# One arm for single shapes in the routed 256-token units: inner branches, moved row turns, split fills and apart last scatters

## The chip, the core and the metric

The kernel runs on one core of a Trainium2 chip. The core has a matrix engine (TensorE, PE in the profile, with PEld for its weight loads), a vector engine (VectorE, DVE), a scalar engine (ScalarE, ACT), GpSimd (POOL) and SyncE (SP), which issues most of the transfers. Each engine has its own instruction stream, and they meet at semaphores. The metric is the device time of one execution in microseconds (us); lower is better.

## What is computed

Three layers follow one another: attention between tokens and states in both directions, a dense feed-forward layer with the mish function, and a layer of eight experts of which each token takes one. The change touches the last:

```python
def _moe2_ref(x, expert_emb, tau, w1, w2):
    xn = x / (np.linalg.norm(x, axis=-1, keepdims=True) + 1e-06)
    en = expert_emb / (np.linalg.norm(expert_emb, axis=-1, keepdims=True) + 1e-06)
    logits = xn @ en.T / tau
    expert_idx = np.argmax(logits, axis=1)
    ...
    gate_w = probs[np.arange(N), expert_idx]
    out = np.zeros((N, D), dtype=np.float32)
    for e in range(E):
        mask = expert_idx == e
        if not mask.any():
            continue
        h = np.maximum(x[mask] @ w1[e], 0.0)
        out[mask] = gate_w[mask, None] * (h @ w2[e])
    return out.astype(np.float32)
```

There are 2304 tokens of 512 numbers, and an expert's w1 is 512 x 1024, its w2 1024 x 512.

## The kernel before

All products are made from two parts of each number, a high and a low one: high by high, high by low and low by high. The routing is worked out on the chip, which sorts the tokens by expert and cuts them into **units** of up to 256 tokens of one expert. Units 0 and 1 are interleaved with the end of the dense layer and the planning; units 2 to 12 run in a loop that is unrolled in the program, each with its own code on each engine. Unit 12 is END; a few more units exist for other routings and are skipped here.

A unit has a *kind*, read from a planned table into a register of each engine. Kind 2 (double) has two blocks of 128 tokens; kind 1 (thick) one block; kind 0 (half) at most 64 tokens, whose high and low parts lie side by side in one block, so that two products suffice and are added at the end. In the profiled execution units 2, 5, 6, 7, 10 and 12 are double, 3, 4, 8, 9 and 11 half, and none is thick. `chosen` is an If over the kind with three arms, once for `up` and once for `out_of`.

The stages of unit U, in program order:

- `gather(U + 2)`: GpSimd issues two indirect transfers (L1052) that fetch the rows `xg` of unit U + 2. It stands behind the scatters of unit U - 1 in GpSimd's queue.
- `up`: the product with w1 into three PSUM tiles `hp`. In a double unit that is four groups of 24 matmuls. In a half unit it is two groups of eight matmuls of 512 columns (`high`, L1173); ScalarE copies each to `hs` (L1216), TensorE turns it with four matmuls against `fold` (L1222, "turn" below; `fold` adds the two halves), and `positive` makes hth (ScalarE L1140, VectorE L74). Near its end, `xt_turns(U + 1)` (L1085) turns the rows of the next unit by eight transposes.
- `next_rows`: ScalarE and VectorE split the turned rows into xth and xtl, then `fill` and `fill_soon` split staged weights: ScalarE writes w1h or w2h (L79), VectorE w1l or w2l (L80), four tiles for w1 and four for w2, according to the planned code `due`. For unit 2 it asks for w1 and w2 of unit 3, for unit 3 for w1 of unit 5, for unit 8 for w2 of unit 9, for unit 9 for w1 and w2 of unit 10. Then `kinds` loads kinds of later units to registers (L1063).
- `out_of`: the product with w2 into `y` (`down` in a double unit, 48 matmuls; 16 matmuls in a half one), `scale` on VectorE (L66), in a half unit a copy of the other lanes on ScalarE (L1243) and an addition on VectorE, and `scatter` on GpSimd (L1155), an indirect transfer to the output.
- `fetch`: SyncE loads the staged weights of later units (L972, L975).

Each engine works through its own stream in order. Scatters of unit END are not issued in the unit but at the very end of the program, after the join of all branches. Between units 0 and 1, `placed` contains the matmuls po (L736) that find each token's place; `group(1, 0)` and `group(1, 1)` before and after it are products of unit 1 (hp, L111 to L113).

Of the kernel before, what the change touches and what calls it, by code (L numbers as in the profile page):

```python
# [21 lines left out]
P = 128  # L22
# [33 lines left out]
def body(tc, x, state, w_in, w_out, ee, tau, w1, w2, out):  # L56
# [58 lines left out]
    with stack:  # L115
# [861 lines left out]
        def split_all(U, parts=(1, 2)):  # L977
            for part in parts:
                for i in range(4):
                    split(*weights(U, part, i), staged[part, i])  # L980
# [73 lines left out]
        kind, kf, due_, hT, HP = {}, {}, {}, [], P // 2  # L1054
        fold = dots.rearrange("p t e -> p (t e)")[:, 0:HP]

        def kinds(U, flag=False):
# [111 lines left out]
        def high(o, terms, last):  # L1169
            n = len(terms)  # L1170
            for low in range(2):
                for k, (h, _, *w) in enumerate(terms):
                    T.matmul(o, h, w[low], start=not low and k == 0, stop=last and bool(low) and k == n - 1)  # L1173

        def low(o, terms):
            n = len(terms)
            for k, (_, l, wh, _) in enumerate(terms):
                T.matmul(o, l, wh, start=False, stop=k == n - 1)

        def sums(o, terms, thick):  # L1180
            high(o, terms, not thick)
            if thick:
                low(o, terms)

        def chosen(U, pieces, do):

            def arm(n):
                for j in range(pieces):
                    do(U, n, j)
# [9 lines left out]
        def up(U, n, j):  # L1199
            def rows_of_next():  # L1200
                if U + 1 in xo:
# [378 lines left out]
```

## Time and profile before

| what | us |
|---|---|
| median of 3 runs (lowest to highest) | 697.71 (697.35 to 698.95) |
| profiled execution | 695.59 |
| its span | 693.8 |
| TensorE busy in the span | 659.0 |
| VectorE busy | 482.6 |
| ScalarE busy | 438.2 |
| GpSimd busy | 184.8 |

The profile comes from one execution. The busy table gives each engine's work; the waits name what ended the idle time before an instruction ("issue" is idle time for which no semaphore stands); the timeline lists instructions in order of start, runs of like ones joined. In a timeline row the first number is the start, the second the time to the end of the group, then engine, line, operation, tile written <- tiles read, shape and count; the bracket at the end is the idle time before it and what ended it. Matmul records overlap: the step from one start to the next is the cost. Rows with a "q" behind the engine are of its sequencer, which reads ahead of the engine.

### The profile page before, as it was taken

Reading aid. Unit: us, or ns where it says so; the run is one execution under the profiler, and the core shown is the slowest. Engines: PE = TensorE matmul, PEld = TensorE weight load, DVE = VectorE, ACT = ScalarE, POOL = GpSimd, SP = SyncE. Lnnn points to the kernel's source line nnn. Section 1 sums busy time; section 2 is a strip of 40 time slices with the busy share of each in tenths; the row PEclk is TensorE's granted clock in tenths of the full one; section 3 lists DMA queues with packets and bytes.
Section 4 is the critical chain, followed back from the end, with each engine's and each line's share of the span. In section 5 each row is a group of like instructions: output and inputs, shape, how many; then the busy total and the mean of one; then the engine's idle time right before and its main releaser. Section 6 shows DMA issues by size and latency. Waiting matters only on the chain. (4 is left out here: it accounts for less than half of the span.)

```text
span 693.8 us, 11871 instructions
## 1 busy us (share of the span) xinstructions
PE 659.0 (95%) x3833; PEld 564.2 (81%) x3833; DVE 482.6 (70%) x1044; ACT 438.2 (63%) x771; POOL 184.8 (27%) x165
## 2 busy tenths in 40 slices
PE   8797999999999999999999999999999999989994
PEld 8787986777888888888887877988978899878893
DVE  5988698889657686686769878897556732467630
ACT  5776998989788867766786677531535521365410
POOL 2776265555000030030004041042121122121101
PEclk9999999999999999999999999999999999999998
DMA  7654044442010154541121354624677281464300
GB/s 182 166 156 122 9 147 125 142 126 62 1 60 1 42 150 97 110 85 38 61 63 49 112 190 162 173 77 158 224 264 280 81 306 62 140 201 175 137 4 34
DMA packets 58243, 82.78 MB, mean 119 GB/s; under 512 B 25050, under 2 KB 35802, under 8 KB 58148
## 3 DMA queue, kind: packets, MB, share of 16 engines
q1 hardware_dynamic: 54388, 70.31, 33.9%
q0 software_dynamic: 3760, 11.30, 5.0%
q8 instruction: 47, 0.77, 0.4%
q14 instruction: 48, 0.39, 0.2%
HBM read 65.32 MB, written 13.65 MB: 114 GB/s over the span
## 5 line engine op out<-in xcount | busy, mean ns | idle before, releaser
L111 PE MATMUL acc<-woh,gh 128*128 128x512 f32 x272 | 108.6, 403 | 3.3 <-ACT gh L79 3.2
L112 PE MATMUL acc<-wol,gh 128*128 128x512 f32 x272 | 107.4, 396 | 0.0
L113 PE MATMUL acc<-woh,gl 128*128 128x512 f32 x272 | 94.0, 399 | 0.9 <-DVE gl L80 0.8
L113 PE MATMUL hp<-xth,w1l 128*128 128x256 f32 x256 | 72.3, 282 | 1.2 <-DVE w1l L80 1.2
L111 PE MATMUL hp<-xth,w1h 128*128 128x256 f32 x256 | 72.3, 282 | 0.5 <-DVE htl L74 0.5
L112 PE MATMUL hp<-xtl,w1h 128*128 128x256 f32 x256 | 72.1, 282 | 0.6 <-DVE xtl L80 0.6
L111 PEld LDWEIGHTS acc<-woh,gh 128*128 128x128 f32 x272 | 51.2, 188 | 16.4 <-ACT gh L79 6.5
L522 ACT ACTIVATE er<-h,mb__104 128x512 f32<-128x512 f32 x68 | 46.5, 684 | 25.5 <-PE h L113 22.0
L113 PEld LDWEIGHTS acc<-woh,gl 128*128 128x128 f32 x272 | 50.5, 188 | 14.8 <-DVE gl L80 4.1
L1140 ACT ACTIVATE hth<-hp 128x512 fp32r<-128x512 f32 (+1 forms) x34 | 17.8, 533 | 66.3 <-PE hp L113 58.6
L112 PEld LDWEIGHTS acc<-wol,gh 128*128 128x128 f32 x272 | 51.2, 188 | 10.1
L1155 POOL DMA_INDIRECT out<-ys,ix x19 | 19.1, 1007 | 150.3 <-DVE ix L1158 70.2
L528 DVE TENSOR_TENSOR er<-er 128x512 f32<-128x512 f32 x56 | 40.3, 719 | 22.4 <-ACT er L522 21.9
L551 ACT ACTIVATE h<-er,mb__104 128x512 f32<-128x512 f32 x68 | 47.3, 695 | 8.3 <-DVE er L528 4.8
L111 PE MATMUL h<-xh,mh 128*128 128x512 f32 x128 | 51.3, 401 | 0.1
L112 PE MATMUL h<-xl,mh 128*128 128x512 f32 x128 | 50.7, 396 | 0.4 <-DVE xl L80 0.4
L113 PE MATMUL h<-xh,ml 128*128 128x512 f32 x128 | 50.5, 394 | 0.0
L552 ACT ACTIVATE er<-er,mb__104 128x512 f32<-128x512 f32 x68 | 49.3, 726 | 1.4
L113 PEld LDWEIGHTS hp<-xth,w1l 128*128 128x128 f32 x256 | 48.4, 189 | 1.8 <-DVE w1l L80 1.8
L112 PEld LDWEIGHTS hp<-xtl,w1h 128*128 128x128 f32 x256 | 48.3, 189 | 1.2 <-DVE xtl L80 0.8
L111 PEld LDWEIGHTS hp<-xth,w1h 128*128 128x128 f32 x256 | 48.3, 189 | 1.1 <-DVE htl L74 0.7
L523 ACT ACTIVATE u<-h 128x512 f32<-128x512 f32 x68 | 40.3, 593 | 0.0
(481 smaller groups left out, 1716.1 us busy)
## 6 DMA issues: line engine op xcount, KB each, us to landing
w<-in_moe_w_in SPq DMA_DIRECT2D x16, 512.0 KB, 3.9
w<-in_moe_w_out SPq DMA_DIRECT2D x16, 512.0 KB, 3.6
es<-in_moe_w SPq DMA_DIRECT2D x32, 256.0 KB, 3.1
sg<-in_moe_w SPq DMA_DIRECT2D x12, 512.0 KB, 3.7
sd<-in_moe_w SPq DMA_DIRECT2D x12, 512.0 KB, 6.5
se<-in_moe_w SPq DMA_DIRECT2D x12, 512.0 KB
xn<-in_x SPq DMA_DIRECT2D x32, 128.0 KB, 3.1
md<-mr SPq DMA_DIRECT2D x28, 128.0 KB, 2.4
```

Of the source, the lines that this page charges most:

```text
L111: T.matmul(o, lh, rh, start=first, stop=False)
L112: T.matmul(o, lh, rl, start=False, stop=False)
L113: T.matmul(o, ll, rh, start=False, stop=last)
L522: A.activation(z, h, AF.Tanh, scale=0.5, bias=mb_[:, 0:1])
L523: A.activation(u, h, AF.Silu)
L528: V.tensor_tensor(out=z, in0=z, in1=z, op=ALU.mult)
L551: A.activation(r, z, AF.Square, scale=QS, bias=mb_[:, 1:2])
L552: behind["ACT"] = A.activation(z, z, AF.Square, scale=QS, bias=mb_[:, 2:3])
L1140: A.activation(hi, i, AF.Relu)
L1155: G.indirect_dma_start(out=out[:, :], out_offset=bass.IndirectOffsetOnAxis(ap=ix_[U][r], axis=0), in_=ys_[U][r], in_offset=None, bounds_ch ...
```

## The change

The thick and the half shape now share an arm: `chosen` has two arms, double and single. In the single arm the matmuls with low parts (`low`), and the choice between transposes and turns with `fold`, stand in small branches of their own. Where the inner branch of `low` is not taken, one matmul of one column with a tile of zeros stands in its place. For these branches TensorE has a second register with the kind, `kp`. The order in the single arm is new: the first turn lies after five of the second group's eight matmuls, the second turn among the first half of the y matmuls, which begin before it.

The turns of the next unit's rows stand at the head of the unit, and if the next unit is not double only those of the first block are made. `fill` is cut in two: the first part (all of w1 for the next unit, half of its w2, or half of the w1 for the unit after) stays in the middle, the second stands after the scatters. Half of `group(1, 1)` moves ahead of `placed`. In unit END the second half's product and scale stand in an If of their own behind the arm.

The diff, cut to its core:

```diff
-        def fill(U):
+        def fill(U, half):
             with tc.If(due_[U] > 1):
-                with tc.If(due_[U] > 2):
-                    split_all(U + 1, [1])
-                split_all(U + 1, [2])
-
-        def fill_soon(U):
-            with tc.If(due_[U] == 1):
-                split_all(U + 2, [1])
+                if not half:
+                    with tc.If(due_[U] > 2):
+                        split_all(U + 1, 1)
+                split_all(U + 1, 2, range(2 * half, 2 * half + 2))
+            if U + 2 <= END:
+                with tc.If(due_[U] == 1):
+                    split_all(U + 2, 1, range(2 * half, 2 * half + 2))
...
                 kind[U] = nc.values_load(cell, engines=UENG, min_val=0, max_val=2)
+                kp[U] = nc.values_load(cell, engines=[ET.PE], min_val=0, max_val=2)
...
         def xt_turns(U, parts=range(2)):
-            for r in range(2):
+            def rows_of(r):
...
+            rows_of(0)
+            if U not in kp:
+                rows_of(1)
+                return
+            with tc.If(kp[U] > 0) as w:
+                rows_of(1)
+            with w.Else():
+                T.matmul(xo[U][1][:, 511:512], wz, wz[:, 0:1], start=True, stop=True, skip_group_check=True)
...
+        def low(U, o, terms):
             n = len(terms)
+            with tc.If(kp[U] > 0) as w:
+                for k, (_, l, wh, _) in enumerate(terms):
+                    T.matmul(o, l, wh, start=False, stop=k == n - 1, skip_group_check=True)
+            with w.Else():
+                T.matmul(o[:, 0:1], wz, wz[:, 0:1], start=False, stop=True, skip_group_check=True)
+
+        def chosen(U, j):
             with tc.If(kind[U] > 1) as w:
-                arm(2)
+                (double_up, double_out)[j](U)
             with w.Else():
-                with tc.If(kind[U] > 0) as v:
-                    arm(1)
-                with v.Else():
-                    arm(0)
+                (single_up, single_out)[j](U)
...
+        def double_out(U):
+            for r in range(1 if U == END else 2):
+                down(U, [r])
+                scale(U, r)
+                scatter(U, r)
...
+            high(hq[U][0], terms(0), True)
+            low(U, hq[U][0], terms(0))
+            leave(0)
+            high(hq[U][1], terms(1), True, range(5))
+            turn(0)
+            high(hq[U][1], terms(1), False, range(5, 8))
+            low(U, hq[U][1], terms(1))
+            leave(1)
+            high(y, ts[0:4], True, range(4))
+            turn(1)
+            high(y, ts[0:4], False, range(4, 8))
+
+        def single_out(U):
+            o, ts = y_[U][0], second(U)
+            high(o, ts[4:8], False)
+            low(U, o, ts)
             scale(U, 0)
...
             group(1, 0)
+            group(1, 1, [0])
             placed()
...
             grouped(1, 0)
-            group(1, 1)
+            group(1, 1, [1])
...
-                    chosen(U, 4, up)
-                    next_rows(U)
+                    if U < END:
+                        xt_turns(U + 1)
+                    chosen(U, 0)
+                    middle(U)
                     if U < END:
                         ends(U)
-                    chosen(U, 2, out_of)
+                    chosen(U, 1)
+                    if U < END:
+                        fill(U, 1)
+                    else:
+                        with tc.If(kind[U] > 1):
+                            down(U, [1])
+                            scale(U, 1)
```

`leave(m)` is the copy to hs on ScalarE, `turn(m)` the four turns and `positive`, and `middle` is the old `next_rows` with the first part of `fill`.

On TensorE, between units 0 and 1, before: the last matmuls of `group(1, 0)` (tile hp_5123) and then those of po.

```order
L111 MATMUL hp_5123<-xth_4981,w1h_4815 128x256
L112 MATMUL hp_5123<-xtl_4982,w1h_4815 128x256
L113 MATMUL hp_5123<-xth_4981,w1l_4816 128x256
L111 MATMUL hp_5123<-xth_4981,w1h_4872 128x256
L112 MATMUL hp_5123<-xtl_4982,w1h_4872 128x256
L113 MATMUL hp_5123<-xth_4981,w1l_4873 128x256
L736 LDWEIGHTS Q
L736 MATMUL po<-ph_5007,Q 128x64
```

The same place after: hp_5124 is the tile of `group(1, 1)`; the last six of its twelve matmuls there are shown.

```order
L111 MATMUL hp_5124<-xth_4981,w1h_4815 128x256
L112 MATMUL hp_5124<-xtl_4982,w1h_4815 128x256
L113 MATMUL hp_5124<-xth_4981,w1l_4816 128x256
L111 MATMUL hp_5124<-xth_4981,w1h_4872 128x256
L112 MATMUL hp_5124<-xtl_4982,w1h_4872 128x256
L113 MATMUL hp_5124<-xth_4981,w1l_4873 128x256
L736 LDWEIGHTS Q
L736 MATMUL po<-ph_5007,Q 128x64
```

Twelve matmuls that stood behind po now stand ahead of it.

On VectorE, around the end of unit 3, before: four splits of w1, then the scale ys of the unit (first that of the double arm, then those of the thick and the half one).

```order
L80 TENSOR_TENSOR w1l_4804<-sg_5331,w1h_4803 128x1024
L80 TENSOR_TENSOR w1l_4810<-sg_5334,w1h_4809 128x1024
L80 TENSOR_TENSOR w1l_4816<-sq,w1h_4815 128x1024
L80 TENSOR_TENSOR w1l_4873<-sr,w1h_4872 128x1024
L1040 UNCONDITIONAL_BRANCH x2
L1028 UNCONDITIONAL_BRANCH
L1191 COMPARE_AND_BRANCH
L1158 CAST ix_6435<-gg_5643 128x1
L66 TENSOR_SCALAR ys_6437<-y_6139,gg_5643 128x512
```

The same place after, from the scale of the single arm on; the splits of sg stand ahead of it as before.

```order
L66 TENSOR_SCALAR ys_6422<-y_6139,gg_5665 128x512
L1253 COMPARE_AND_BRANCH
L74 SCALAR_TENSOR_TENSOR ys_6422<-hs_6147,gg_5665,ys_6422 64x512
L1253 UNCONDITIONAL_BRANCH x2
L1193 UNCONDITIONAL_BRANCH
L1032 COMPARE_AND_BRANCH
L80 TENSOR_TENSOR w2l_4676<-se_5333,w2h_4675 128x1024
L80 TENSOR_TENSOR w2l_4710<-se_5336,w2h_4709 128x1024
L1032 UNCONDITIONAL_BRANCH x2
L1038 COMPARE_AND_BRANCH
L80 TENSOR_TENSOR w1l_4816<-sq,w1h_4815 128x1024
L80 TENSOR_TENSOR w1l_4873<-sr,w1h_4872 128x1024
```

The splits of sq and sr, and the last two of w2 where these are due, have moved behind the scale.

On GpSimd, at the end of the program, before: the last two scatters and what follows, with their waits.

```order
L1549 UNCONDITIONAL_BRANCH
L1155 DMA out_0<-yse0_10163,dots_183 2176x512 [waits DMASW4_49,DMASW3_49,DMASW5_49,DMASW2_49,DMASW6_49,DMASW1_49,DMASW7_49,DMASW0_49,DVE_49]
L1155 DMA out_0<-yse1_10164,dots_183 2176x512 [waits DMASW3_49,DMASW2_49]
L1576 UNCONDITIONAL_BRANCH
L1576 ISA [waits barrier_Pool_Activation_PE_DVE_SP_gather]
```

After:

```order
L1570 UNCONDITIONAL_BRANCH
L1163 DMA out_0<-yse0_9854,dots_183 2176x512 [waits DMASW4_49,DMASW3_49,DMASW5_49,DMASW2_49,DMASW6_49,DMASW1_49,DMASW7_49,DMASW0_49,DVE_49]
L1163 DMA out_0<-yse1_9855,dots_183 2176x512 [waits DMASW3_49,DMASW2_49,DVE_49]
L1597 UNCONDITIONAL_BRANCH
L1597 ISA [waits barrier_Pool_Activation_PE_DVE_SP_gather]
```

The order is the same; the second scatter has got a wait for VectorE of its own.

## Rows read from the trace of the kernel before

**Rows 1.** The page's busy table: busy us, share of the span, instructions.

```profile
PE 659.0 (95%) x3833; PEld 564.2 (81%) x3833; DVE 482.6 (70%) x1044; ACT 438.2 (63%) x771; POOL 184.8 (27%) x165
```

**Rows 2.** Waits of TensorE, 480 to 694 us: releaser, total, times, longest.

```profile
PE hp L1173 <- issue: 3.2, 2, 1.7
PE hp L1173 <- DVE w1l L80: 1.5, 1, 1.5
PE hp L113 <- DVE w1l L80: 1.2, 3, 0.5
```

**Rows 3.** Timeline of the end of unit 12: scales and scatters.

```profile
678.00 0.75 DVE L66 TENSOR_SCALAR yse<-y,gg 128x512 f32<-128x512 f32 x1 [4.56 <-PE y L113]
...
683.58 0.75 DVE L66 TENSOR_SCALAR yse<-y,gg 128x512 f32<-128x512 f32 x1 [4.77 <-PE y L113]
684.61 0.98 POOL L1155 DMA_INDIRECT out<-yse,dots  x1 [20.46 <-DVE yse L66]
687.94 0.98 POOL L1155 DMA_INDIRECT out<-yse,dots  x1 [2.35 <-DMA out<-yse,dots]
```

**Rows 4.** Sequencer rows (ns min/median/max), 540 to 544 us; unit 5's first y.

```profile
L1063 PEldq TENSOR_LOAD <-ctl x2: 296/296/297, 541.5 to 542.2; - x2
L1191 PEldq COMPARE_BRANCH  x2: 73/186/298, 541.1 to 542.9; - x2
...
543.10 0.48 PE L111 MATMUL y<-w2h,hth 128*128 128x512 f32 x1
```

**Rows 5.** Timeline of TensorE at po.

```profile
460.22 0.28 PE L112 MATMUL hp<-xtl,w1h 128*128 128x256 f32 x1
460.34 0.28 PE L113 MATMUL hp<-xth,w1l 128*128 128x256 f32 x1
461.92 0.66 PE L736 MATMUL po<-ph,Q 128*128 128x64 bf16 x17 [1.30 <-DVE ph L66]
```

**Rows 6.** Timeline of units 8 and 9: turns, row turns, copies, splits.

```profile
605.02 1.00 PE L1222 MATMUL hp<-dots,hs 128*128 128x64 f32 x8
...
605.85 1.04 PE L1085 MATMUL gt<-ident,xg 128*128 128x128 f32 x8
...
606.53 0.42 DVE L74 SCALAR_TENSOR_TENSOR hth<-hp,hth 128x256 fp32r<-128x256 f32 x1 [4.30 <-ACT hth L1140]
...
606.74 1.00 PE L1222 MATMUL hp<-dots,hs 128*128 128x64 f32 x8
...
610.59 1.98 ACT L79 ACTIVATE w2h<-se 128x1024 fp32r<-128x1024 f32 x2
...
615.91 0.59 ACT L1243 ACTIVATE hs<-y 64x512 f32<-64x512 f32 x1 [3.34 <-DVE ys L66]
...
616.53 0.60 ACT L1216 ACTIVATE hs<-hp 128x512 f32<-128x512 f32 x1
...
617.33 1.00 PE L1222 MATMUL hp<-dots,hs 128*128 128x64 f32 x8
```

**Rows 7.** Windows of units 3, 4, 8, 9: length, engines' busy times, clock.

```profile
506.80:517.29 10.49, 10.45 (x57) 8.37 (x55) 2.51 (x9) 3.29 (x8) 3.00 (x3) 1.00 0.90 320
518.78:530.91 12.13, 10.59 (x57) 8.68 (x57) 8.20 (x14) 7.27 (x12) 3.62 (x4) 1.00 0.92 337
601.28:611.79 10.51, 10.47 (x57) 8.36 (x55) 4.17 (x9) 5.42 (x10) 2.97 (x3) 1.00 0.44 153
613.49:623.93 10.44, 10.40 (x57) 8.62 (x57) 6.24 (x12) 6.02 (x10) 2.94 (x3) 1.00 0.71 233
```

**Rows 8.** Unit 2's second scatter, unit 5's gather, their transfers' time.

```profile
503.81 2.35 DVE L80 TENSOR_TENSOR w2l<-se,w2h 128x1024 fp32r<-128x1024 f32 x2
...
514.84 1.00 POOL L1155 DMA_INDIRECT out<-ys,ix  x1 [6.35 <-DVEq L1033]
...
517.44 2.02 POOL L1052 DMA_INDIRECT xg<-x1d,perm  x1 [0.30 <-PE y L1173]
...
xg<-x1d,perm POOLq DMA_INDIRECT x2, 7.2
```

**Rows 9.** Sequencer row of TensorE at the end of unit 3.

```profile
L1191 PEldq COMPARE_BRANCH  x1: 3827/3827/3827, 514.3 to 514.3; - x1
```

More of the change, by code (lines that the diff above doesn't have):

```diff
@@ L975, in fetch_part, with split_all @@
                     Y.dma_start(staged[2, i].rearrange("p (t d) -> p t d", t=2), src)
[L977 to L980, printed above, removed]
+        def split_all(U, part, tiles=range(4)):
+            for i in tiles:
+                split(*weights(U, part, i), staged[part, i])
         def expert(s, engines):
@@ L1167, in lanes, with high @@
             return t.rearrange("p (k t) -> p k t", t=P)[:, :, half * HP : (half + 1) * HP]
-        def high(o, terms, last):
+        def high(o, terms, first, steps=None):
             n = len(terms)
[L1171 to L1175, printed above, removed]
+            for i in steps or range(2 * n):
+                h, _, *w = terms[i % n]
+                T.matmul(o, h, w[i // n], start=first and not i, stop=False, skip_group_check=True)
@@ L1218, in up @@
-            for k in range(4):
-                if n:
-                    T.transpose(tr[:, k * P : (k + 1) * P], h[:, k * P : (k + 1) * P], ident)
-                else:
-                    T.matmul(tr[:, k * P : k * P + HP], h[:, k * P : (k + 1) * P], fold, start=True, stop=True)
-            if n:
-                positive(hth[U][m], htl[U][m], tr)
-            else:
-                positive(lanes(hth[U][m], 0), lanes(hth[U][m], 1), lanes(tr, 0))
-            if j == 2:
-                rows_of_next()
@@ L1230, in out_of @@
-        def out_of(U, n, j):
-            if n > 1:
-                down(U, [j])
-                scale(U, j)
-                scatter(U, j)
-                return
-            if j:
-                return
-            q, o = U % 2, y_[U][0]
-            sums(o, [(hth[U][k // 4][:, k % 4 * P : (k % 4 + 1) * P], htl[U][k // 4][:, k % 4 * P : (k % 4 + 1) * P], W2H[q, k // 2][:, k % 2, :], W2L[q, k // 2][:, k % 2, :]) for k in range(NFE)], n)
+        def double_out(U):
[3 more added lines that the diff above has]
+                scatter(U, r)
@@ new lines, in second, with single_up, terms, leave @@
+        def second(U):
+            q = U % 2
+            return [(hth[U][k // 4][:, k % 4 * P : (k % 4 + 1) * P], htl[U][k // 4][:, k % 4 * P : (k % 4 + 1) * P], W2H[q, k // 2][:, k % 2, :], W2L[q, k // 2][:, k % 2, :]) for k in range(NFE)]
+        def single_up(U):
+            q, y, ts = U % 2, y_[U][0], second(U)
+            h, tr = hs_[U], (hq[U][2], hq[U][0])
+            def terms(m):
+                fs = slice(m * 512, (m + 1) * 512)
+                return [(*(wide2(t[U][k // 2])[:, k % 2, 0:P] for t in (xth, xtl)), W1H[q, k][:, fs], W1L[q, k][:, fs]) for k in range(KT)]
+            def leave(m):
+                A.activation(h[m], hq[U][m], AF.Copy)
+            def turn(m):
+                with tc.If(kp[U] > 0) as w:
+                    for k in range(4):
+                        T.transpose(tr[m][:, k * P : (k + 1) * P], h[m][:, k * P : (k + 1) * P], ident)
+                with w.Else():
+                    for k in range(4):
+                        T.matmul(tr[m][:, k * P : k * P + HP], h[m][:, k * P : (k + 1) * P], fold, start=True, stop=True)
+                with tc.If(kf[U] > 0) as w:
+                    positive(hth[U][m], htl[U][m], tr[m])
+                with w.Else():
+                    positive(lanes(hth[U][m], 0), lanes(hth[U][m], 1), lanes(tr[m], 0))
+            high(hq[U][0], terms(0), True)
[9 more added lines that the diff above has]
+            high(y, ts[0:4], False, range(4, 8))
@@ L1507, in body @@
             kinds(2)
-            next_rows(1)
+            middle(1)
             store(1)
+            fill(1, 1)
             fetch(1)
@@ L1540, in body @@
                         fetch_part(e, part)
-                    split_all(U)
+                    for part in (1, 2):
+                        split_all(U, part)
                     xt_tiles(U)
```

41 lines of the change are left out of this document (8 added, 33 removed).

## Prediction

> **What bounds the kernel now.** I read the busy table first, then the waits of TensorE in the stage of the 256-token units (480 to 694 us), then the timeline where units meet and where the program ends. TensorE is busy for 95% of the span [rows 1]. From 480 us on its waits are few: two stalls put down to "issue" (3.2 us), and waits for split weights of 1.5 and 1.2 us [rows 2]. So in this stage a microsecond that TensorE gains or loses reaches the end, and after TensorE's last matmul at about 683.5 us only the tail counts: scale, scatter, transfer. The profiled execution took 695.59 us, of which 693.8 us are the span; the median of the runs shown is 697.71 us, 2.12 us more. I make the sum against 695.59 and add the same 2.12 at the end.
>
> **The tail.** Unit 12 is a double one: its first half of 128 rows is scaled at 678.00, its second at 683.58 [rows 3]. Still both scatters leave after the second: GpSimd issues the first at 684.61, having waited 20.46 us for VectorE, and the second at 687.94, having waited for the first's transfer [rows 3]. In the order of the new kernel the second scatter has a wait of its own for VectorE, so the first waits for its own scale only. It then leaves at about 678.00 + 0.75 + 0.28 = 679.03, where 0.28 is the step from the end of the second scale (683.58 + 0.75 = 684.33) to 684.61. With the same 3.33 us from issue to issue (687.94 - 684.61) GpSimd is free at 682.36, before 684.61. The second scatter takes the first's place: **-3.33 us**, with 2.25 us of cover. The new branch between the halves is read by TensorE's sequencer ahead of its queue, so I count it at nothing; without that cover it is one taken branch, at most 0.3 us [rows 4]. The bounds are 0 and -3.33.
>
> **The placement matmuls.** At 461.92 TensorE starts po after idling 1.30 us for ph on VectorE [rows 5]. Twelve hp matmuls are moved ahead of it, 0.12 us apart [rows 5], 1.43 us in all, so they fill the hole, and po starts when it did. No wait of TensorE lies between 462 and the first unit's end that could swallow the gain: **-1.30 us** (bounds 0 and -1.30).
>
> **Register loads.** Each `kinds` now loads the kind twice on TensorE. A load, its check and its move take 0.7 us start to start on the sequencer (two of them from 541.5 and 542.2) [rows 4]. In unit 5 the compare that follows starts at 542.9 and lasts up to 298 ns, and y starts at 543.10 [rows 4]: there is no slack. Units 2 and 5 read two kinds each, so two more loads. In a double unit the sequencer is some 2 us ahead (first branch at 541.1, y at 543.10), which the loads and branches use up: **+1.4 us each**. Units 6 and 7 read one kind: the slack was 0.7 us and one more load uses it, 0. In half units the queue ahead is longer (512-column matmuls at (683.58 - 678.00)/24 = 0.23 us): 0. The bounds for each of the two units are 0 and 1.4; I take 1.4 because of the missing slack.
>
> What the trace shows of such a load is 296 ns, then 146 to 151 ns more and a check. The Trainium skill ("Runtime: NRT & Kernel Launch", section Instruction fetch mechanics) puts a register load at about 200 ns; by that figure alone, an estimate from the page, each unit would lose 0.4 us and the forecast would be some 2 us lower. The trace disagrees with it here, and I follow the trace.
>
> **Row turns.** They move to the head of the unit, and only four of eight remain where the next unit is a half one. Eight cost 606.74 - 605.85 = 0.89 us [rows 6]. The next unit is a half one in units 2, 3, 7, 8 and 10: -0.44 us in each. That gives unit 2 +0.95 with its loads and **unit 7 -0.44**.
>
> **Body of a half unit.** Before, U8 takes 10.51 us [rows 7]: 16 hp and 16 y matmuls at 0.23 (7.44), two turns at 605.85 - 605.02 = 0.83, row turns 0.89, so waits of about 0.5. New are three one-column matmuls where the inner branch is not taken. No such row stands in the trace; one lies between 0 and the 0.23 of a 512-column one, and I take 0.1, since the turn's short ones take 0.83/8. Branches on the sequencer are 73 to 298 ns [rows 4], five pairs in 10 us, hidden by the queue. From a turn's start to its hth the trace has 606.53 + 0.42 - 605.02 = 1.93 us [rows 6]. After turn(0) TensorE now has 0.83 + 3 x 0.23 + 0.1 = 1.6 us of work, after turn(1) 0.83 + 4 x 0.23 = 1.76: waits of 0.3 and 0.2, as much as before. So a half unit gains 0.44 and pays 0.3 (-0.15) before a half one, and pays 0.3 before a double one. **Unit 11: +0.4** (its next is double).
>
> **Units 8 and 9.** Before, TensorE's stall at the start of unit 9 (611.79 to 613.49 [rows 7]) cost less than it looks, for turn(0) of unit 9 waited on ScalarE anyway: hs of the left half of hp at 616.53 + 0.60, turn(0) at 617.33 [rows 6], which is 5.54 us after unit 8's last y. ScalarE was late because L1243 waits for VectorE's scale [rows 6], which stands behind the w2l splits. Now two of the four splits come after the scatter, so on ScalarE two w2h (2.0 us [rows 6]) stand between L1243 and that hs. Counted from the end of unit 8's turn(1): VectorE ends xth and two w2l at about 4.9 (0.38 for hth, 0.9 for xth, 2.0 for w2h, then VectorE's part); the scale takes 0.75, L1243 0.6, w2h 2.0, hs 0.6, hand-overs 0.25, so turn(0) is possible at 9.1. y ends at 3.0 (12 matmuls, 0.3 of rest), so turn(0) comes 6.1 us after it: +0.56. The rest of unit 9 was 623.93 - 617.33 = 6.60 and is now the sum of its pieces, 6.76. With unit 8's -0.15: **+0.6 us**. The removed stall does not come back as a gain.
>
> **Units 3 and 4.** The pair took 530.91 - 506.80 = 24.11 us, units 8 and 9 took 22.65 [rows 7]. By the pattern above the new pair would take 23.2, -0.9. But two things are late here. The staged weights arrive late, and the row turns of unit 5 now stand first in unit 4, at about 517. Their rows are fetched by the gather at 517.44, which follows the second scatter at 514.84; the transfers take 7.2 us in the middle [rows 8], so the rows are there at about 524.6; behind the row turns the whole unit 4 is queued on TensorE. That scatter in turn waits for the first, and the first for a scale that stands behind w2l, which ends at 503.81 + 2.35 [rows 8]. Two of these splits, 2.36 us, now come after the scale, so the gather leaves some 2.4 us earlier, and more if its scatter meets fewer weight loads: about 518 to 523. ScalarE allows turn(0) at about 524 anyway, 3.1 us after the row turns (eight hp, a small one, five hp), and the last four row turns take 0.44: this covers rows landing up to 520.5. I take **+0.3 us**, between -0.9 and +4.4 (gather no earlier than before).
>
> **Unit 10.** Weights for it are split in unit 9 and TensorE waited for them (1.2 us [rows 2]). The splits now start 3.0 instead of 4.1 us before the end of y, four row turns (0.44) fill part: the wait grows 0.6, eight turns go (-0.89), four come (+0.44): **+0.15 us**.
>
> **Sum.** -1.30 + 0.95 + 0.3 + 1.4 - 0.44 + 0.6 + 0.15 + 0.4 = +2.06 on TensorE, -3.33 in the tail: -1.27. The profiled execution becomes 694.3, the median 696.4 us. TensorE's end moves from 683.5 to about 685.6.
>
> **Rivals.** (A) The costs are covered: loads at nothing (-2.8), no late ScalarE in units 4 and 9 (-0.6 and -1.2). For it: the queue ahead of the sequencer may be deeper in the new order, and the row turns no longer stand at its end. Against: the y start right behind the compare [rows 4]. 696.4 - 4.6 = 691.8. (B) Slower: unit 4 waits at its head for the gathered rows of unit 5. If they land at 524.6 as before, turn(0) comes at 528.1, 4.1 us past my figure: 700.5. It decides from a landing after 520.5 on. For it: the transfers ran while weight loads filled the DMA queues; against: the earlier scale. (C) The change doesn't do what it says, the first last-half scatter still waits for both: without -3.33, 699.7. Against it stands the second scatter's own wait in the order. (D) A jump over the double arm waits for its code: the branch at 514.3 took 3827 ns where others took 73 to 298 [rows 4, 9], and TensorE stood 1.5 us. If units 3, 8 and 11 paid that too, 4.5 us: 700.9. Against: it happened only in the second of two half units in a row, and only one arm is jumped now. The Trainium skill (same page and section) says that a taken branch out of the two pages held forces a fetch; the row at 514.3 agrees. By that rule a shorter arm makes such waits rarer.
>
> **How the numbers follow.** The forecast has 0.45, A 0.2, B 0.2, C 0.07, D 0.08. A difference of 0.2% (1.4 us) is about what a measurement of this kernel tells from none. The forecast lies at -1.3, so half of its 0.45 is faster, nearly all of the rest within 0.2%; A is faster. Some of B, half absorbed, ends within. Faster 0.43, within 0.31, slower 0.26. The range reaches to A and B and leaves D and the ends of A out: 692.0 to 700.5.
>
> **What would show it.** The profile after should have: no idle before po; two scatters of the last unit, the first before TensorE's end, the second about 1.1 us after; y of units 2 and 5 with an idle of some 1.4 us ahead named issue; turn(0) of units 4 and 9 waiting for ScalarE; gaps at the head of unit 4 only if B holds. I would be wrong if units 2 and 5 run without that gap, or if gathers or code fetches stop TensorE at other heads.

## The result: slower

The changed kernel takes 702.66 us in the median of 12 runs, the kernel before 697.25 us in 12 runs beside it. The ratio is 1.010, with an interval from 1.0071 to 1.013. The forecast was 696.4 us and no gain beyond 1.3 us; the time lies above the range.

Single executions spread over 4 us and more, most of it before unit 2: TensorE began unit 2 at 480.79 us in the trace of the changed kernel, at 483.19 in that of the kernel before, at 487.76 in the last run below. So I compare the lengths of units on TensorE, from a unit's first instruction to that of the next; an idle stretch ahead of the first belongs to the unit it delays.

| stretch | before | after | predicted change | measured change |
|---|---|---|---|---|
| unit 2 | 23.61 | 24.52 | +0.95 | +0.91 |
| units 3 and 4 | 24.11 | 26.40 | +0.3 | +2.3 |
| unit 5 | 23.46 | 25.24 | +1.4 | +1.8 |
| unit 6 | 23.45 | 23.80 | 0 | +0.35 |
| unit 7 | 23.46 | 23.34 | -0.44 | -0.1 |
| units 8 and 9 | 22.65 | 28.15 | +0.6 | +5.5 |
| unit 10 | 26.21 | 27.31 | +0.15 | +1.1 |
| unit 11 | 10.33 | 11.08 | +0.4 | +0.75 |
| tail: TensorE's end to the span's end | 10.3 | 6.8 | -3.3 | -3.4 |

The last row is 693.8 - 683.54 and 700.5 - 693.67. Of the 12.6 us that units 2 to 11 lost, 5.5 are in units 8 and 9.

These are the waits of TensorE in the changed kernel from 450 us on (what waited, for what, total us, times, longest), which answer to [rows 2], and the row of the page with the granted clock in 40 slices of the span:

```profile
PE y L111 <- ACT xth L79: 2.4, 2, 1.3
PE gt L1084 <- DMA xg<-x1d,perm: 2.4, 2, 1.9
PE hp L1230 <- ACT hs L1222: 2.0, 1, 2.0
PE hp L113 <- DVE w1l L80: 1.5, 3, 0.5
PE hp L1181 <- issue: 1.2, 1, 1.2
PE y L1181 <- DVE hth L74: 0.9, 4, 0.2
```

```profile
PEclk9989999999999999999999999999999999989999
```

The first wait is that of units 2 and 5 ahead of y, the second the row turns at the head of unit 4, the third turn(0) of unit 9. The waits add up to 10.4 us, against 5.9 us in [rows 2] and the one of 1.30 us before po in [rows 5]. That is not enough for the 12.6 us by which units 2 to 11 became longer.

The windows of units 3, 4, 8 and 9 and of two stretches in them (length, then busy time and count of PE, PEld, DVE, ACT and POOL, then the granted clock, the DMA share and GB/s) answer to [rows 7] and show the rest:

```profile
505.31:516.21 10.90, 10.62 (x57) 8.14 (x55) 5.47 (x10) 4.31 (x8) 3.52 (x4) 1.00 0.69 236
516.21:531.71 15.50, 12.81 (x60) 9.52 (x60) 7.53 (x14) 6.98 (x11) 3.00 (x3) 0.89 0.83 304
604.09:614.85 10.76, 10.48 (x57) 8.08 (x56) 5.49 (x10) 4.32 (x8) 3.92 (x3) 1.00 0.51 173
614.85:632.24 17.39, 14.18 (x61) 10.95 (x61) 8.21 (x14) 7.03 (x11) 3.97 (x3) 0.80 0.49 155
519.26:526.00 6.74, 6.74 (x28) 5.20 (x29) 3.11 (x3) 3.30 (x5) 3.00 (x3) 0.75 1.00 366
...
622.52:630.00 7.48, 7.48 (x27) 6.34 (x28) 0.87 (x3) 1.71 (x4) 1.92 (x2) 0.54 0.70 221
```

The granted clock was 1.00 in all four units in this execution of the kernel before. Now it is 0.75 from 519.26, behind the wait for gathered rows, and 0.54 from 622.52, behind the wait for ScalarE: TensorE ran at its lower level, 1.2 GHz, for half of the first stretch and for most of the second.

The parts that I had held for sure are there. In the timeline of the changed kernel po follows hp without an idle bracket, and the two last scatters leave apart, the first before TensorE's end and the second 1.03 us after its scale begins, as in [rows 3] the first one did:

```profile
461.02 0.66 PE L736 MATMUL po<-ph,Q 128*128 128x64 bf16 x17
```

```profile
688.12 0.75 DVE L66 TENSOR_SCALAR yse<-y,gg 128x512 f32<-128x512 f32 x1 [4.46 <-PE y L113]
...
689.15 0.98 POOL L1163 DMA_INDIRECT out<-yse,dots  x1 [14.82 <-DVE dots L1166]
693.70 0.75 DVE L66 TENSOR_SCALAR yse<-y,gg 128x512 f32<-128x512 f32 x1 [4.77 <-PE y L113]
694.73 0.98 POOL L1163 DMA_INDIRECT out<-yse,dots  x1 [4.60 <-DVE yse L66]
```

The timeline of the changed kernel where unit 8 ends and unit 9 begins, which answers to [rows 6]:

```profile
613.87 2.36 DVE L80 TENSOR_TENSOR w2l<-sd,w2h 128x1024 fp32r<-128x1024 f32 x2 [0.61 <-ACT w2h L79]
...
617.09 1.17 PE L1181 MATMUL hp<-w1h,xth 128*128 128x512 f32 x4 [1.17 <-issue]
...
617.79 0.15 DVE L1166 CAST ix<-gg 128x1 int32<-128x1 f32 x1 [1.56 <-issue]
...
618.72 0.59 ACT L1255 ACTIVATE hs<-y 64x512 f32<-64x512 f32 x1 [3.94 <-PE hp L1181]
...
619.22 1.99 ACT L79 ACTIVATE w2h<-se 128x1024 fp32r<-128x1024 f32 x2
...
621.87 0.60 ACT L1222 ACTIVATE hs<-hp 128x512 f32<-128x512 f32 x1 [0.66 <-ACTq L1038]
622.52 1.79 PE L1230 MATMUL hp<-dots,hs 128*128 128x64 f32 x8 [2.05 <-ACT hs L1222]
```

This is the chain I had predicted: splits, scale of unit 8, copy of its lanes, two w2h, hs, turn(0). It ends 622.52 - 614.85 = 7.67 us after unit 8's last y; I had 6.1. VectorE finishes its splits at 616.23 and then idles 1.56 us ahead of the scale, for nothing that a semaphore shows. The sequencer rows tell what lies there: one of VectorE's register loads in this unit after, the same one before, and VectorE's last splits and its instruction ahead of the scale in the kernel before.

```profile
L1061 DVEq TENSOR_LOAD <-ctl x1: 300/300/300, 616.8 to 616.8; - x1
```

```profile
L1063 DVEq TENSOR_LOAD <-ctl x1: 298/298/298, 613.2 to 613.2; - x1
```

```profile
612.03 2.35 DVE L80 TENSOR_TENSOR w2l<-se,w2h 128x1024 fp32r<-128x1024 f32 x2
615.00 0.15 DVE L1158 CAST ix<-gg 128x1 int32<-128x1 f32 x1 [0.61 <-DVEq L1040]
```

Before, the loads stood ahead of the second If (`fill_soon`) and ran while VectorE was still splitting; the new `fill` holds both Ifs and stands ahead of the loads, which now begin when the splits are done. After turn(0) unit 9 takes 9.72 us instead of 6.76.

### The profile page after: what moved, and what is told of

Its sections match the earlier page's. It is cut to its first block, busy times and chain, and to the rows that moved or that the text cites. A ratio compares the mean times of both kernels' runs of the same rounds, so it can differ in the third digit from the quotient of the medians.

```text
span 700.5 us, 12053 instructions
## 1 busy us (share of the span) xinstructions
PE 668.0 (95%) x3833; PEld 568.8 (81%) x3833; DVE 482.5 (69%) x1044; ACT 438.1 (63%) x771; POOL 188.8 (27%) x165
## 5 line engine op out<-in xcount | busy, mean ns | idle before, releaser
L1163 POOL DMA_INDIRECT out<-ys,ix x19 | 22.3, 1176 | 158.8 <-DVE ix L1166 70.6
L111 PE MATMUL y<-w2h,hth 128*128 128x512 f32 x96 | 38.6, 403 | 2.8 <-ACT xth L79 2.4
```

What stands on the lines that cost most here:

```text
L111: T.matmul(o, lh, rh, start=first, stop=False)
L1163: G.indirect_dma_start(out=out[:, :], out_offset=bass.IndirectOffsetOnAxis(ap=ix_[U][r], axis=0), in_=ys_[U][r], in_offset=None, bounds_ch ...
```

## The experiments

The three groups of runs come from different chips, so each time is given with its ratio to the kernel before, run beside it on the same chip. Unit lengths are those of the profiled execution. The first four runs were built to take the two waits and the clock apart, and to price the two sure parts by themselves.

**Fill in one piece** (e1, on the changed kernel):

```diff
+            if half:
+                return
             with tc.If(due_[U] > 1):
-                if not half:
-                    with tc.If(due_[U] > 2):
-                        split_all(U + 1, 1)
-                split_all(U + 1, 2, range(2 * half, 2 * half + 2))
+                with tc.If(due_[U] > 2):
+                    split_all(U + 1, 1)
+                split_all(U + 1, 2)
             if U + 2 <= END:
                 with tc.If(due_[U] == 1):
-                    split_all(U + 2, 1, range(2 * half, 2 * half + 2))
+                    split_all(U + 2, 1)
```

> The changed kernel with fill in one piece again, in the middle of the unit; all else as changed. Theory (split fill makes ScalarE late for turn(0) of unit 9): no splits of w2h stand between the copy of unit 8's lanes and hs of unit 9, so turn(0) of unit 9 comes about 6.5 us after unit 8's last y instead of 7.7, and the idle before it falls from 2.05 to about 1; unit 4 pays up to 2.4 us more, since unit 2's first scale is late again and with it the gather for unit 5. Net between -3 and +2 us against the changed kernel. Rival (the order inside the single arm is what makes ScalarE late, not the split of fill): turn(0) of unit 9 stays at 7.7 us behind unit 8's last y.

709.76 us, 1.0166 of the kernel before (1.0107 to 1.0224): slower still. My theory on unit 9 fell. Without any split between them turn(0) comes 631.13 - 623.70 = 7.43 us after unit 8's last y, near the 7.67 of the rival, and the wait grew to 3.03 us. What the split fill does is elsewhere: without it unit 2's second scatter leaves at 516.49 (509.63 in the changed kernel), and the row turns at the head of unit 4 stand for 10 us. Rows of this run's timeline, of TensorE at units 4 and 9 and of GpSimd:

```profile
527.64 2.30 PE L1085 MATMUL gt<-ident,xg 128*128 128x128 f32 x8 [10.33 <-DMA xg<-x1d,perm]
...
631.13 1.97 PE L1231 MATMUL hp<-dots,hs 128*128 128x64 f32 x8 [3.03 <-ACT hs L1223]
```

```profile
516.49 1.87 POOL L1164 DMA_INDIRECT out<-ys,ix  x1 [7.26 <-DMA out<-ys,ix]
```

So the split of fill is what kept my rival B small. Units 3 and 4 took 34.5 us here.

**Row turns later** (e2, on the changed kernel):

```diff
-                    if U < END:
-                        xt_turns(U + 1)
                     chosen(U, 0)
+                    if U < END:
+                        xt_turns(U + 1)
                     middle(U)
```

> The changed kernel with the row turns of the next unit moved from the head of the unit to behind the up stage; all else as changed. Theory (row turns at the head wait for gathered rows): the waits of 0.52 and 1.90 us at the head of unit 4 are gone, the granted clock stays at 1.00 there, units 3 and 4 together fall from 26.4 us to about 24.5; units 2 and 5 still wait for register loads. About -2 us against the changed kernel. Rival (unit 4 is held by ScalarE or by code fetches as well): the pair stays within 0.7 us of 26.4.

709.75 us, 1.016 (1.0111 to 1.0209). The waits for gathered rows are gone, as expected, yet units 3 and 4 took 28.5 us: an idle of 2.58 us named issue, up to 521.13, took their place in unit 4, and the clock fell again (0.72 in the unit). I take this idle for a code fetch; no long branch stands beside it, so that is not shown. In unit 9 turn(0) waited 4.50 us for ScalarE, 626.90 - 618.46 = 8.4 us after unit 8's last y: with the row turns behind half of y, the splits begin later still. The rival holds in direction, and it pointed to the order inside the arm.

**Work in the idle stretches** (e3, on the changed kernel): `pad(U, n)` issues n matmuls of 512 columns into a tile that turn(0) overwrites.

```diff
+                    if U == 4:
+                        pad(U, 10)
                     if U < END:
                         xt_turns(U + 1)
...
             high(hq[U][1], terms(1), True, range(5))
+            if U == 9:
+                pad(U, 9)
             turn(0)
```

> The changed kernel with matmuls into a scratch PSUM tile whose result is not used: ten ahead of the row turns in unit 4, nine ahead of turn(0) in unit 9 (2.3 and 2.1 us at full clock), where TensorE idled. Theory (the fall of the granted clock follows these idle stretches): the clock stays at 1.00 from 520 to 530 and from 620 to 635 us, the matmuls there take 0.23 us again, and the program becomes 3 to 5 us faster although it has more work. Rival (the clock falls for another reason, or the time was lost in the waits alone): the same time as the changed kernel, within 1 us, or slower by up to 4.4 us, and the clock falls at the same places.

702.06 us, 1.0061 (1.0029 to 1.0092). With 19 matmuls more the kernel is not slower; the ratio is 0.4% lower than that of the changed kernel, but the intervals overlap. Its windows of units 4 and 9, and the stretches behind the waits:

```profile
518.94:533.94 15.00, 13.73 (x71) 10.35 (x71) 7.67 (x14) 6.99 (x11) 3.00 (x3) 1.00 0.82 302
...
617.07:631.88 14.81, 13.18 (x70) 10.06 (x70) 8.21 (x14) 7.04 (x11) 3.97 (x3) 1.00 0.55 181
522.89:529.60 6.71, 6.39 (x33) 4.88 (x34) 3.19 (x4) 3.47 (x5) 3.00 (x3) 1.00 1.02 376
624.74:632.00 7.26, 6.98 (x38) 5.37 (x39) 3.17 (x8) 4.07 (x7) 1.92 (x2) 1.00 0.71 222
```

The clock is 1.00 throughout. Turn(0) of unit 9 comes at the same distance from unit 8's last y (624.74 - 617.07 = 7.67), the rest of the unit takes 631.88 - 624.74 = 7.14 instead of 9.72. So the low clock in unit 9 costs 2.6 us. That it follows the idle stretch is borne out by the other traces with the new order in the arm: the five without these matmuls (the changed kernel, e1, e2, e5, e6) have a granted clock of 0.72 to 0.89 in unit 4 and of 0.72 to 0.82 in unit 9. The idle of 1.17 us in unit 9 did not happen in this run, and turn(0) came no earlier: it was covered by ScalarE. The gain of 3 to 5 us that I had expected in the time of the program is not shown.

**The tail and po alone** (e4, on the kernel before):

```diff
             if n > 1:
+                if U == END and j:
+                    return
                 down(U, [j])
...
             group(1, 0)
+            group(1, 1, [0])
             placed()
...
-            group(1, 1)
+            group(1, 1, [1])
...
                     chosen(U, 2, out_of)
+                    if U == END:
+                        with tc.If(kind[U] > 1):
+                            down(U, [1])
+                            scale(U, 1)
```

> The kernel before with only two parts of the change: the last unit's second half in a branch of its own, and half of group(1, 1) ahead of the placement matmuls. Theory (these two are free of cost): 3.3 us from the tail and 1.3 us from the gap before po, so about 692.6 us, 4.6 us under the kernel before. Rival (the tail's gain is given back by the new branch or the gap before po only moves): 695 to 697 us.

693.53 us, 0.9908 (0.9876 to 0.994), 5.0 us under the kernel before beside it. These two parts are worth what was forecast; the rest of the change costs what they gain and more. The loop's half units are those of the kernel before, yet the clock fell in this execution too. Its windows of units 4 and 9:

```profile
517.57:531.85 14.28, 12.03 (x56) 9.93 (x57) 9.65 (x15) 8.81 (x14) 4.95 (x4) 0.88 0.90 335
...
612.72:626.53 13.81, 11.96 (x57) 9.80 (x58) 7.98 (x14) 6.83 (x11) 2.94 (x3) 0.88 0.61 195
```

They follow stalls of 1.87 and 1.81 us at the heads of these units, and units 8 and 9 took 24.3 us together, 1.65 more than in the table above. So up to that much of the +5.5 can lie between two executions of the same code.

The second four followed three suspects: the kind loads, VectorE's idle ahead of the scale, and the order of the single arm.

**Kind loads at the end of the unit** (e5, on the changed kernel):

```diff
-                kp[U] = nc.values_load(cell, engines=[ET.PE], min_val=0, max_val=2)
+        def kinds_pe(U):
+            kp[U] = nc.values_load(ctl[0:1, 1, U : U + 1], engines=[ET.PE], min_val=0, max_val=2)
...
                     chosen(U, 1)
+                    for u in AHEAD.get(U, ([], []))[0]:
+                        kinds_pe(u)
```

> The changed kernel with TensorE's second load of each kind moved from the middle of the unit to its end, behind the product with w2 (48 matmuls of 0.23 us in a double unit). Theory (the second loads cost TensorE 1.2 us in units 2 and 5 each, and are hidden behind the long matmuls): the idle of 1.28 and 1.14 us ahead of y in units 2 and 5 goes, about -2.4 us against the changed kernel. Rival (y waits there for something else, as the row reads ScalarE's xth): the two idles stay, same time within 0.7 us.

703.31 us, 1.005 (1.0022 to 1.0078). Both idles ahead of y are gone: unit 2 takes 23.33 us (24.52 in the changed kernel), unit 5 24.19 (25.24). The theory holds, although the waits of TensorE name ScalarE's xth there: that is the last semaphore of a matmul whose engine was held by its sequencer. But unit 4 took 18.32 us (15.50), with two waits of 2.2 us at its row turns: TensorE came earlier, the gathered rows did not. Unit 10 took 26.25 us here, with the new order in the arm, at a granted clock of 1.00.

**Loads ahead of the splits** (e6, on the changed kernel):

```diff
-            if U < END:
-                xt_split(U + 1)
-                fill(U, 0)
             for u in AHEAD.get(U, ([], []))[0]:
                 kinds(u)
             for u in AHEAD.get(U, ([], []))[1]:
                 dues(u)
+            if U < END:
+                xt_split(U + 1)
+                fill(U, 0)
```

> The changed kernel with the register loads of the middle ahead of the splits and not behind the second If of fill. Theory (VectorE's loads stand behind a join that waits until its splits are done, so the scale comes 1.5 to 2.1 us after the last split): the idle named issue ahead of ix in units 2 and 8 falls from 2.15 and 1.56 us to about 0.3, the gather of unit 5 leaves nearly 2 us earlier, the wait at the head of unit 4 falls from 2.4 to under 1 us, turn(0) of unit 9 comes 1.0 to 1.5 us earlier behind unit 8's last y (now 7.67); the clock falls less; -3 to -6 us against the changed kernel. Rival (VectorE's idle is a code fetch): the idle stays and the time too.

706.24 us, 1.0096 (1.0068 to 1.0124): no gain. Two rows of its timeline in unit 8, of VectorE and ScalarE:

```profile
623.36 0.15 DVE L1166 CAST ix<-gg 128x1 int32<-128x1 f32 x1 [0.41 <-DVEq L1038]
```

```profile
618.87 0.45 ACT L79 ACTIVATE xth<-gt 128x128 fp32r<-128x128 f32 x2 [1.26 <-issue]
```

The idle ahead of ix fell from 1.56 to 0.41 us, so the loads behind the join were the cause of most of it and not a code fetch. But now ScalarE loads ahead of xth and idles 1.26 us there; the splits start as much later, and turn(0) comes 628.08 - 620.20 = 7.9 us after unit 8's last y. The wait at the head of unit 4, which I had expected under 1 us, grew to 4.77. The cause of the idle was right, the gain was not.

**The old order in the arm** (e7, on the changed kernel):

```diff
-            high(hq[U][1], terms(1), True, range(5))
-            turn(0)
-            high(hq[U][1], terms(1), False, range(5, 8))
+            high(hq[U][1], terms(1), True)
             low(U, hq[U][1], terms(1))
             leave(1)
-            high(y, ts[0:4], True, range(4))
+            turn(0)
             turn(1)
-            high(y, ts[0:4], False, range(4, 8))
...
-            high(o, ts[4:8], False)
+            high(o, ts, True)
```

> The changed kernel with the matmuls of the single arm in the order of the kernel before: all of hp, both turns, then all 16 of y; row turns stay at the head, fill stays split. Theory (with half of y ahead of the middle, the splits start 1.1 us later as seen from the end of y, and this alone makes ScalarE late in unit 9): turn(0) of unit 9 comes about 6.5 us after unit 8's last y, not 7.67, at the price of up to 0.5 us a half unit; -1 to -3 us against the changed kernel. Rival (the order inside the arm does not matter to ScalarE): turn(0) stays at 7.67 and the time is the same or up to 2 us longer.

696.12 us, 0.9938 (0.9906 to 0.9971): 1.6% lower than the changed kernel's ratio, by this edit alone. Unit 9 takes 11.98 us instead of 17.39, unit 10 26.07 instead of 27.31. Turn(0) in this run's timeline with VectorE's idle ahead of the scale, and the window of unit 9:

```profile
615.12 0.15 DVE L1166 CAST ix<-gg 128x1 int32<-128x1 f32 x1 [1.54 <-issue]
...
619.59 2.00 PE L1230 MATMUL hp<-dots,hs 128*128 128x64 f32 x16 [0.83 <-ACT hs L1222]
```

```profile
613.80:625.78 11.98, 10.95 (x61) 8.66 (x60) 8.02 (x13) 8.12 (x13) 3.96 (x3) 1.00 0.72 223
```

Turn(0) comes 619.59 - 613.80 = 5.79 us after unit 8's last y, the wait is 0.83 us, and the clock stays at 1.00. The rest of the unit takes 6.19 us; three matmuls of hp, 0.7 us, now stand ahead of turn(0) and not behind it. The price of the old order is in the half units that a half one follows: 11.07 us for unit 8 against 10.76, 11.11 for unit 3 against 10.90.

**All three** (e8): the edits of e5, e6 and e7 together.

> The changed kernel with the three edits together: second kind loads at the unit's end, loads ahead of the splits, and the old order in the single arm. If each takes away its own wait they add up: -7 to -10 us against the changed kernel, 693 to 696 us. If they share one cause (the late splits), the sum is no better than the best alone, -3 to -6 us. Against the kernel before with only the tail and the placement matmuls changed (693.5 us), anything below 692 would show that the shared arm is worth its price.

698.14 us, 0.9982 (0.9955 to 1.0009), no better than the old order alone. They do not add up. Units 2 and 5 are short (23.3 and 23.9 us), but the row turns of unit 4 waited 6.34 us, and unit 9 took 14.07 us.

The last four put together what had held, with the kernel of e4 run again beside them.

**Old order and late kind loads** (e9): the edits of e5 and e7.

> The changed kernel with the old order in the single arm and TensorE's second kind loads at the unit's end; row turns stay at the head, fill stays split, loads of the other engines stay where the change has them. Theory (the order of the arm and the loads are separate losses): units 2 and 5 fall by 1 us each and unit 9 stays near 12.0 us; but the gather of unit 5 does not come earlier, so unit 4 gives back up to 1.2 us at its head. 1 to 2 us under the old order alone, about 0.991 of the kernel before. Rival (the loads at the end delay the next head): no gain over the old order alone.

696.95 us, 0.9987 (0.9952 to 1.0023). Units 2 and 5 fall to 23.45 and 23.72 us and unit 9 stays at 12.59, but unit 4 takes 17.93 us:

```profile
520.42 2.30 PE L1086 MATMUL gt<-ident,xg 128*128 128x128 f32 x8 [4.41 <-DMA xg<-x1d,perm]
```

TensorE gets to unit 4 earlier and stands there longer. I had allowed 1.2 us for it; unit 4 took 3.6 more than in e7 (17.93 against 14.33). The wait grew by 1.84 (4.41 against 2.57), and the granted clock of the unit was 0.81 against 1.00.

**And the row turns back** (e10): the edits of e2, e5 and e7.

> As the kernel with the old order in the arm and the later kind loads, and the row turns also behind the up stage, about where they were before. Theory (row turns at the head matter through the gather of unit 5 alone): unit 4 has no wait for gathered rows, units 3 and 4 together take about 24 us instead of 25.4; but the splits start 0.5 to 0.9 us later as seen from the end of y, so turn(0) of unit 9 comes later by as much. About 0.989 of the kernel before. Rival (what the splits lose is worth more than the gather's wait): slower than with the row turns at the head.

691.38 us, 0.9899 (0.9865 to 0.9933). The waits for gathered rows are gone. Units 3 and 4 take 10.33 and 12.58 us, 22.9 together; unit 9 takes 14.25, its clock at 0.88. The windows of units 4 and 9:

```profile
514.31:526.89 12.58, 10.63 (x62) 8.47 (x61) 7.31 (x13) 6.71 (x10) 3.00 (x3) 1.00 1.02 378
...
608.74:622.99 14.25, 12.23 (x59) 10.14 (x60) 8.49 (x14) 8.61 (x13) 3.97 (x3) 0.88 0.59 189
```

**And fill in one piece** (e11): the edits of e1, e2, e5 and e7.

> As the last one, with fill in one piece in the middle: of the change there remain the shared arm with its small branches, four row turns ahead of half units, the tail and the placement matmuls. Theory (with the old order, splitting fill no longer decides): within 1 us of the last one, and within 2 us of the kernel before with only the tail and the placement matmuls changed. Rival (the shared arm itself costs): 3 us or more slower than that one.

695.94 us, 0.9966 (0.993 to 1.0003), 4.6 us over e10: the split of fill is worth its place once the order of the arm is the old one. Unit 4 took 17.63 us here and unit 9 15.72. It lies 2.35 us above the kernel of e12, between what the theory and the rival allowed.

**The tail and po again** (e12).

> The kernel before with only the tail and the placement matmuls changed, run again beside the others so that they can be compared on one chip: 0.991 of the kernel before, as the first time, within 0.003.

693.59 us, 0.9934 (0.9901 to 0.9967); the first time it was 0.9908. In this execution the stalls at the heads of units 4 and 9 were 1.96 and 1.53 us, and the granted clock stayed at 1.00 in both units, where it had been 0.88 in e4. This kernel, e7 and e10 beat the kernel before and the changed one. Between this one and e10, 0.9934 and 0.9899, the intervals overlap: that e10 is the better one is not shown.

## Why the prediction was wrong

**What held.** The tail (-3.33 predicted, -3.4 measured), the hole before po (1.30 us, gone), the kind loads in unit 2 (+0.95 and +0.91), and that they and nothing else hold y there (e5). That +0.95 and +0.91 lie so close is in part luck: without the second loads unit 2 takes 23.33 us, so these cost 1.2 and not 1.4, and the rest of the unit gained 0.28 (23.61 - 23.33) and not 0.44. The Trainium skill's 200 ns a register load ("Runtime: NRT & Kernel Launch", Instruction fetch mechanics) would have given, as an estimate, +0.4 less the row turns; the trace's own load row was the better guide. The 0.4 us a place that this page would have counted came to 1.2 (24.52 - 23.33).

**The step that failed: units 8 and 9.** I gave +0.6, and it was +5.5. The path was the right one, ScalarE's hs for turn(0) behind unit 8's scale, but three terms of the sum were wrong. First, turn(0) was to come 6.1 us after unit 8's last y and came after 7.67. I had the scale following the splits at once; VectorE's register loads stand between them, behind a join that lets them begin only when the splits are done: 1.56 us of idle, 0.41 with the loads moved ahead (e6). Second, TensorE's clock: I priced the rest of unit 9 at full speed, 6.76 us. After idles of 1.17 and 2.05 us the granted clock was 0.54 and the rest took 9.72; at 1.00 it took 7.14 (e3), so the clock cost 2.6. Third, the body of unit 8 was put at -0.15 and came out at +0.25. These are 1.57 + 2.96 + 0.40, the 4.9 us by which the sum fell short.

What makes the chain late is the new order of the arm. I never set it against the old one; it enters the sum only as the 3.0 us left behind the middle. Four traces hold it apart from the split of fill, to which I had put the +0.56. The table gives the microseconds from unit 8's last y to turn(0) of unit 9:

| | fill whole | fill split |
|---|---|---|
| old order | 5.54 (kernel before) | 5.79 (e7) |
| new order | 7.43 (e1) | 7.67 (changed kernel) |

The split of fill costs 0.25 us, the order 1.9 (the kernel before also has its row turns behind up). VectorE's idle of 1.54 us is still there in e7, but the work behind up starts earlier. ScalarE's first xth begins 613.80 - 609.50 = 4.3 us ahead of unit 8's end there, and 614.85 - 612.16 = 2.7 in the changed kernel:

```profile
609.50 0.44 ACT L79 ACTIVATE xth<-gt 128x128 fp32r<-128x128 f32 x2
```

```profile
612.16 0.44 ACT L79 ACTIVATE xth<-gt 128x128 fp32r<-128x128 f32 x2
```

Taking the order back gives 5.4 us back in unit 9 (e7), the clock's 2.6 among them.

**Units 3 and 4.** +0.3 predicted, +2.3 measured, inside the bounds of -0.9 and +4.4. The second gather left 512.23 - 505.31 = 6.9 us after the start of unit 3, before 517.44 - 506.80 = 10.6: 3.7 us earlier and not 2.4. Still TensorE stood at the row turns, 0.52 us for the first block and 1.90 for the second. Rows of TensorE and ScalarE:

```profile
516.73 0.63 PE L1084 MATMUL gt<-ident,xg 128*128 128x128 f32 x4 [0.52 <-DMA xg<-x1d,perm]
...
519.26 0.66 PE L1084 MATMUL gt<-ident,xg 128*128 128x128 f32 x4 [1.90 <-DMA xg<-x1d,perm]
...
520.87 1.04 ACT L79 ACTIVATE w1h<-sr 128x1024 fp32r<-128x1024 f32 x1
```

Most of this wait was covered, as I had said: ScalarE split w1h until 521.91, which with 0.6 for hs and a hand-over of 0.15 allows turn(0) at about 522.7, and the row turns, over at 519.9, allow it 3.1 us later, at 523.0. It came at 524.66. What was not covered is the clock of 0.75 behind the wait: eight hp matmuls took 3.15 us (519.89 to 523.04) instead of 1.9. Rival B was thus half right: the place and the cause of the idle, not its price. That the idle would be far longer as soon as unit 2 became shorter (e5, e8, e9), or fill whole (e1), I had not seen.

**Unit 5**: +1.4 predicted, +1.8 measured, of which the loads are 1.05 (e5). The rest I did not trace. **Unit 6**: +0.35 where I had 0; with the row turns back behind the up stage it is 23.46 and 23.45 us (e2, e10), so it goes with their place. **Unit 10**: +1.1 instead of +0.15, with a granted clock of 0.83 in the ten microseconds from 630. It is 26.07 us with the old order (e7), but 26.25 with the new order at a clock of 1.00 (e5); so it is not the order alone, and what the clock did there is not told apart. **Bodies of half units**: unit 8 +0.25 instead of -0.15, unit 11 +0.75 instead of +0.4. Cutting hp into five and three and y into four, four and eight costs about 0.1 us at each new piece (the first four matmuls of a piece took 1.02 us, the next four 0.94), which I had left out. With the row turns behind the up stage the two units take 10.60 and 10.80 us with the cuts (e2) and 10.38 and 10.37 without (e10): the cuts cost 0.2 and 0.4, and the row turns at the head 0.2 and 0.3. **Unit 7**: I gave -0.44 for four row turns that fall away, and -0.1 came.

**The rivals.** A (covered costs) is refuted by units 2 and 5. B came true in part. C is refuted by the two scatters. D, a jump that holds TensorE up, happened once and cost nothing: the branch at 615.4, ahead of unit 9, took 1.53 us and TensorE idled 1.17, but ScalarE came later. In e10 a branch of 4.67 us left TensorE idle for 1.95 in unit 4. The 1.5 us that I had put to the branch at 514.3 are, by [rows 2], a wait for VectorE's w1l; it ended at 518.78, after the branch (514.33 + 3.83 = 518.16). That the change would become slower through the clock was in none of them.

What stays open: why the clock fell to 0.88 in units 4 and 9 of e4 and not in the kernel before and e12, whose half units are the same and whose stalls were 1.49 to 1.96 us; why it fell in unit 9 of e10 with a wait of 1.26 us; and whether e10 is faster than e4.

## What to carry to other kernels

An order that leaves one engine's waits unchanged can still move the starting line of the others: count the work that stands behind the point where the helpers start, on every engine, before calling a reordering neutral. Moving a consumer forward is worth only as much as its producer's lead; where the producer is an indirect transfer behind two others, every gain ahead of it turns into a wait at that place. Parts with one clear mechanism and no new wait (here the tail and the placement matmuls) are best measured by themselves first, since they may carry the whole gain of a bundle.

## What the runs showed of the hardware

- The granted clock of TensorE fell behind idle stretches: to 0.75 after 0.52 and 1.90 us in unit 4, to 0.54 after 1.17 and 2.05 us in unit 9; with matmuls of no use in these stretches it stayed at 1.00 (e3). The length of a stall alone does not tell: with the half units of the kernel before, stalls of 1.87 and 1.81 us were followed by a fall (0.88 in each unit, e4), stalls of 1.96 and 1.53 us in another execution of the same kernel were not (e12), nor 1.49 and 1.70 in the kernel before, nor 2.57 at the head of unit 4 in e7. An idle stretch can so cost twice: the 2.05 us in unit 9 went with 2.6 us more.
- Register loads of VectorE and ScalarE cost 1.56 us where they stand behind a join and 1.26 where they stand ahead of the first instruction (rows above); the idle is named "issue". Where they run while the engine still works, 0.61 us of idle is left (kernel before).
- A wait that the trace puts down to an engine can be the sequencer's own time: y of unit 2 "waited for ScalarE" for 1.28 us, and the wait went with a register load (e5).
